# First expert layer with its weight blocks stationary at run-time addresses, instead of tokens stationary

## The chip, the cores and the metric

The kernel runs on one core of a Trainium2 chip. The metric is the device time in microseconds (us), median of several executions. A ratio compares a kernel with the kernel before on the same chip, and uses fast runs only; where numbers of two chips stand side by side, the text says so. With one core, "slow" only means a run more than 1.5% above the fastest run of the same kernel. For a kernel whose runs spread more widely, the fast ratio therefore flatters, and the median of all runs is given beside it.

## The reference, cut to what matters

```python
# attention with random features: q, k, v are 8 batches x 8 heads x 576 x 64
# -> x, 8 x 576 tokens of D = 512
e = argmax(x @ w_gate)                 # or the token before's expert, if a local gate says so
h = np.maximum(x[b, s] @ w1[e], 0.0)   # w1: 8 experts x 512 x 1024
out[b, s] = p[e] * (h @ w2[e])         # w2: 8 experts x 1024 x 512
```

Each token goes to one of eight experts. Which one is known only at run time. (The code in this document is shortened; `...` marks what is left out.)

## The kernel before

After attention the tokens are sorted by expert into pages of 128 tokens; 38 pages are computed. A page gathers its tokens (`xg`), turns them so that D lies on the partitions (`xt`), and loads the column offset of its expert, `ev`, into a register of TensorE. All of w1 and w2 is to lie in SBUF: `w1_all` and `w2_all`, 4,096 columns (`WE`) for each expert. There `ds(ev + ..., n)` is a slice at a run-time address. In the traces a matmul is two instructions: a weight load (LDWEIGHTS) and the matmul itself; layer 1 before has 304 LDWEIGHTS `<-xt` and as many MATMUL `pj<-w_all,xt` (291 of them recorded). The operand of the weight load is called the stationary one here (`lhsT`), the other the moving one (`rhs`).

```python
def hidden(n, xt, ev_src, mid=lambda: None):             # layer 1 of a page
    ev = nc.values_load(ev_src, engines=(PE,), ...)
    h_ps = ...                                           # PSUM, 128 tokens x 1024 units
    for c in range(2):
        for dc in range(DC):                             # DC = 4
            nc.tensor.matmul(h_ps[:, c, :], lhsT=xt[:, dc, :],                  # stationary: tokens
                             rhs=w1_all[:, ds(ev + (dc * F + c * 512), 512)],   # moving: weights
                             start=(dc == 0), stop=(dc == DC - 1))
        if c == 0:
            mid()                                        # transposes of the next page's tokens
    h = arena[:, n % 3].rearrange(...)
    nc.scalar.activation(h, h_ps..., Act.Relu)           # tokens on the partitions
    return h, ev

def hidden_t(h, n=FC):                                   # FC = 8: units onto the partitions
    ...                                                  # tp in PSUM, ht in SBUF
    for f in range(n):
        nc.tensor.transpose(tp[:, f], h[:, f], ident_bf)
    nc.vector.tensor_copy(ht[:, 0:n], tp[:, 0:n])
    if n < FC:
        nc.sync.dma_start_transpose(out=ht[:, n:], in_=h[:, n:]...)
    return ht, n_
```

Layer 2 (`output`) is eight matmuls with a 128x128 block of `ht` stationary and 512 columns of w2, also at a run-time address, moving. The first 17 pages do layer 1 only, while w2 is still being loaded (three loads of `w_load` per page); then both layers alternate. Routing ("gate", with one-hot tables built on VectorE) is done twice, once for each half of the tokens.

The softmax here doesn't subtract the row's maximum and nothing guards it: scores larger than these inputs give would overflow.

Of the kernel before, what the change touches and what calls it, by code (L numbers as in the profile page):

```python
# [23 lines left out]
NEP = 18  # L24
# [6 lines left out]
def kernel(  # L31
# [118 lines left out]
    def w_load():  # L150
        if wload and wdst[wload[0][0]] is not None:
            l, e, i = wload.pop(0)
            src = (moe_w1, moe_w2)[l]
            w = src.shape[2]
            nb = 1024 // w
            nc.gpsimd.dma_start(  # L156
                out=wdst[l][:, ds(e * WE + i * 1024, 1024)].rearrange("p (c f) -> p c f", f=w),
                in_=src[e].rearrange(("(c p) f -> p c f", "(p c) f -> p c f")[l], p=128)[:, i * nb:(i + 1) * nb, :])
# [170 lines left out]
    ids2 = consts.tile([128, 18, 2], BF)  # L329
    wt8 = consts.tile([128, E], F32)  # L330
    io128 = consts.tile([128, 128], BF)
# [9 lines left out]
    def gate_consts():  # L341
# [3 lines left out]
        nc.gpsimd.iota(io128, pattern=[[1, 128]], base=0, channel_multiplier=0, **fdt)  # L345
# [11 lines left out]
        nc.gpsimd.iota(ids2[:, :, 0].rearrange("p (a r) -> p a r", a=2), pattern=[[128, 2], [0, 9]], base=0,  # L357
                       channel_multiplier=1, **fdt)
        nc.gpsimd.iota(ids2[:, :, 1].rearrange("p (a r) -> p a r", a=2), pattern=[[0, 2], [1, 9]], base=1,
                       channel_multiplier=0, **fdt)  # L360
        nc.gpsimd.iota(wt8, pattern=[[-1, E]], base=E, channel_multiplier=0, **fdt)
        nc.gpsimd.iota(cpg, pattern=[[1, NC]], base=0, channel_multiplier=0, **fdt)
        yield
# [18 lines left out]
    def gate(ep, gt, n):  # L382

# [73 lines left out]
        slf, col = t18("slf"), t18("col")  # L457
        nc.vector.tensor_copy(slf, slot)
        if ep == 0:
            nc.vector.tensor_copy(col, gpg)  # L460
        else:
            nc.vector.tensor_scalar(col, gpg, scalar1=float(NEP), scalar2=over, op0=Alu.is_ge, op1=Alu.mult)
            nc.vector.tensor_tensor(col, col, gpg, op=Alu.add)
# [4 lines left out]
        oh, pg = t18("oh", 128, BF), t18("pg", NC, BF)  # L468
        ri = gt.tile([128, n, 2, NC], BF, name="ri")

        def parts(r_, v_, t_):
            shape = list(r_.shape)
            nc.vector.tensor_tensor(r_, pg[:, t_].unsqueeze(2).to_broadcast(shape), v_[:, t_].unsqueeze(3).to_broadcast(shape),
                                    op=Alu.mult)

        def build(g):
            t_ = slice(n * g, n * g + n)
            nc.vector.tensor_tensor(oh[:, t_], io128.unsqueeze(1).to_broadcast([128, n, 128]),
                                    slf[:, t_].to_broadcast([128, n, 128]), op=Alu.is_equal)
            nc.vector.tensor_tensor(pg[:, t_], cpg.unsqueeze(1).to_broadcast([128, n, NC]),  # L480
                                    col[:, t_].to_broadcast([128, n, NC]), op=Alu.is_equal)
            parts(ri, ids2, t_)
# [4 lines left out]
        for g in range(18 // n):  # L487
            for i in range(n):
                nc.tensor.matmul(l_ps.rearrange("p a c -> p (a c)"), lhsT=oh[:, n * g + i],
                                 rhs=ri[:, i].rearrange("p a c -> p (a c)"),  # L490
                                 start=(g == 0 and i == 0), stop=(n * g + i == 17))
            yield
            if n * (g + 1) < 18:
# [36 lines left out]
        lists[ep] = dict(idr=idr, ix=ix, lid=lid, tmp=(ex, fr, m_, rs, oh, pg, parts))  # L530

    def both(ep, n):
        yield from gate(ep, gt, n)
        yield from probs(ep, gt)

    def probs(ep, gt):

        ex, fr, m_, rs, oh, pg, parts = lists[ep].pop("tmp")
# [5 lines left out]
        v3, pr = t18("v3", 3, BF), t18("pr")  # L544
        rp = gt.tile([128, 6, 3, NC], BF, name="rp")
# [5 lines left out]
        for i in range(2):  # L551
            nc.vector.tensor_copy(v3[:, :, i:i + 1], pr)
            nc.vector.tensor_tensor(v3[:, :, 2:3] if i else pr, pr, v3[:, :, i:i + 1], op=Alu.subtract)
# [4 lines left out]
        for g in range(3):  # L558
            parts(rp, v3, slice(6 * g, 6 * g + 6))
            yield  # L560
            for i in range(6):
                nc.tensor.matmul(p_ps.rearrange("p a c -> p (a c)"), lhsT=oh[:, 6 * g + i],
                                 rhs=rp[:, i].rearrange("p a c -> p (a c)"),
# [40 lines left out]
    outs, hs, done, spare = [], {}, [], list(range(3, 9))  # L604
    NST = 2 * NEP + 2

    def hidden(n, xt, ev_src, mid=lambda: None):
        ev = nc.values_load(ev_src, engines=(PE,), min_val=0, max_val=(E - 1) * WE,
                            skip_runtime_bounds_check_because="multiples of the columns of one expert")
        h_ps = ps_p.tile([128, 8, 128], F32, name="pj").rearrange("p (a x) c -> p a (x c)", a=2)  # L610
        for c in range(2):
            for dc in range(DC):
                nc.tensor.matmul(h_ps[:, c, :], lhsT=xt[:, dc, :], rhs=w1_all[:, ds(ev + (dc * F + c * 512), 512)],  # L613
                                 start=(dc == 0), stop=(dc == DC - 1))
            if c == 0:
                mid()
        h = arena[:, n % 3].rearrange("p (f c) -> p f c", c=128)
        nc.scalar.activation(h, h_ps.rearrange("p a x -> p (a x)").rearrange("p (c f) -> p f c", f=FC), Act.Relu)  # L618
        return h, ev

    def hidden_t(h, n=FC):

        tp = ps_t.tile([128, FC, 128], BF, name="tp")
        for f in range(n):
            nc.tensor.transpose(tp[:, f], h[:, f], ident_bf)  # L625
        n_ = spare.pop(0) if spare else 0
# [243 lines left out]
```

## Time and profile before

| | before |
|---|---|
| time, median | 333.0 us |
| profiled span; mean granted clock of TensorE | 330.9 us; 0.903 |
| first layer-1 matmul | 155.9 us |
| first layer-2 matmul | 217.8 us |
| start of the last matmul | 320.9 us |
| layer-1 and layer-2 matmuls at full clock, start to start | 216 ns each |

Two lines of the page of the kernel before. The first is the granted clock in forty slices of the span, in tenths (9 is 90% or more). The second is the group of layer-1 matmuls: count, then busy time and mean ns of one, then the idle time ahead of them.

```profile
PEclk9859779999899959555799997999999999999996
...
L613 PE MATMUL pj<-w_all,xt 128*128 x291 | 75.2, 389 | 2.6 <-ACT xt L599 1.4
```

In the second half of the span the clock is full nearly throughout, and layer 1 has almost no idle time ahead of it (2.6 us in all). The mean of 389 ns is the latency of a pipelined matmul, whose end the profile models; the pace is the distance between starts, 216 ns. (13 of the 304 records are missing.)

### The profile page before, as it was taken

What the parts mean: (1) busy time and instruction counts of PE and PEld (TensorE: products, weight loads), DVE (VectorE), ACT (ScalarE), POOL (GpSimd) and SP (SyncE); (2) the same over time, 40 slices, a digit from 0 to 9 for tenths busy, and PEclk for the clock granted to TensorE, in tenths of its full rate; (3) what the DMA queues carried; (4) which work ended last, traced back from release to release, by engine and by line L of the source; (5) the groups of instructions that cost most, each with busy time, mean ns of one, the idle gap of its engine ahead of it and who ended that gap; (6) DMA issues with size and microseconds to landing.
All of it is one profiled execution on the core that took longest, in us unless ns stands there. A gap on an engine that the chain in (4) does not pass through costs nothing. (4 is left out here: it accounts for less than half of the span.)

```text
span 330.9 us, 7843 instructions
## 1 busy us (share of the span) xinstructions
PE 257.2 (78%) x2789; PEld 151.7 (46%) x2809; DVE 183.2 (55%) x406; ACT 154.1 (47%) x230; POOL 195.8 (59%) x299
## 2 busy tenths in 40 slices
PE   2585488768787775722998885999999999999980
PEld 1464256546464553411565453554444444444430
DVE  2677188788879768980354776423333333323440
ACT  1586498888889865510555452532122221222000
POOL 3677787698498595356377653325555657432550
PEclk9859779999899959555799997999999999999996
DMA  7999989999888789999689996338668666532330
GB/s 230 391 411 408 315 238 326 368 271 301 285 239 259 239 150 202 224 223 222 130 167 206 226 226 164 81 82 184 171 173 176 189 148 171 168 112 79 129 133 32
DMA packets 52649, 69.89 MB, mean 211 GB/s; under 512 B 25552, under 2 KB 27088, under 8 KB 52608
## 3 DMA queue, kind: packets, MB, share of 16 engines
q0 software_dynamic: 14176, 31.14, 42.4%
q1 hardware_dynamic: 34352, 33.43, 30.9%
q10 hardware_dynamic: 4080, 4.77, 4.2%
q8 instruction: 26, 0.43, 0.5%
q14 instruction: 15, 0.12, 0.1%
HBM read 67.16 MB, written 14.68 MB: 247 GB/s over the span
## 5 line engine op out<-in xcount | busy, mean ns | idle before, releaser
L613 PE MATMUL pj<-w_all,xt 128*128 x291 | 75.2, 389 | 2.6 <-ACT xt L599 1.4
L618 ACT ACTIVATE arena<-pj 128x1024 bf16<-128x1024 f32 x38 | 38.9, 1023 | 75.3 <-PE pj L613 70.9
L644 POOL DMA_INDIRECT out_dram<-y,idr x38 | 37.8, 995 | 51.3 <-DVE y L643 47.3
L584 POOL DMA_INDIRECT xg<-x_tok,ix x36 | 37.4, 1038 | 27.3 <-PE tp L597 16.5
L212 DVE TENSOR_REDUCE kmx<-pj 128x8 f32<-128x1024 f32 x36 | 44.0, 1222 | 16.1 <-ACT kvb L251 8.4
L232 POOL TENSOR_TENSOR va<-vs,ek 128x512 bf16<-128x512 f32 (+1 forms) x40 | 38.2, 958 | 21.0 <-ACT ek L221 15.3
L156 POOL DMA_DIRECT2D w_all<-in_moe_w_dram x64 | 35.8, 565 | 16.4 <-DMA w_all<-in_moe_w_dram 15.3
L281 ACT ACTIVATE qp<-pj 128x1024 bf16<-128x1024 f32 x36 | 37.5, 1043 | 12.4 <-PE pj L275 12.3
L613 PEld LDWEIGHTS <-xt 128*128 128x128 bf16 x304 | 29.0, 99 | 30.2 <-issue 2.2
L218 ACT ACTIVATE kp<-pj 128x1024 bf16<-128x1024 f32 x36 | 37.3, 1037 | 11.2 <-DVE kmx L212 11.2
L643 DVE TENSOR_SCALAR y<-po,prb 128x512 f32<-128x512 f32 x24 | 18.0, 751 | 29.0 <-PE po L638 29.0
L183 PE MATMUL tp<-ident_bf,kb 128*128 128x128 bf16 x144 | 17.1, 246 | 17.1 <-POOL kb L110 8.1
L206 PE MATMUL pj<-om_bd,kt 128*128 128x256 bf16 x144 | 25.8, 310 | 2.9 <-ACT qp L281 1.8
L305 DVE TENSOR_TENSOR xr<-po,rd 128x512 bf16<-128x512 f32 x36 | 24.9, 692 | 1.2
L599 ACT COPY xt<-tp 128x512 bf16<-128x512 bf16 x18 | 10.5, 584 | 30.2 <-PE tp L597 29.1
L638 PE MATMUL po<-w_all,ht 128*128 x103 | 24.5, 379 | 0.1
L628 DVE COPY ht<-tp 128x1024 bf16<-128x1024 bf16 (+1 forms) x20 | 11.9, 597 | 22.5 <-PE tp L625 22.5
L116 POOL CAST qb<-arena 128x512 bf16<-128x512 f32 x36 | 21.1, 612 | 3.9 <-DMA arena<-in_q_dram 3.9
L729 ACT COPY qt<-tp 128x512 bf16<-128x512 bf16 x36 | 21.6, 601 | 3.6 <-DVE kt L727 2.7
L638 PEld LDWEIGHTS <-ht 128*128 128x128 bf16 x160 | 15.1, 98 | 16.1
L628 DVE COPY arena<-tp 128x512 bf16<-128x512 bf16 (+1 forms) x18 | 9.2, 514 | 22.0 <-PE tp L625 22.0
L727 DVE COPY kt<-tp 128x512 bf16<-128x512 bf16 x36 | 15.0, 417 | 11.3 <-PE tp L183 11.2
(152 smaller groups left out, 394.7 us busy)
## 6 DMA issues: line engine op xcount, KB each, us to landing
w_all<-in_moe_w_dram POOLq DMA_DIRECT2D x64, 256.0 KB, 7.9
vs<-in_v_dram SPq DMA_DIRECT2D x8, 1152.0 KB, 12.5
arena<-in_q_dram SPq DMA_DIRECT2D x4, 2304.0 KB, 15.1
ks<-in_k_dram SPq DMA_DIRECT2D x7, 1152.0 KB, 13.8
x_tok<-xr ACTq DMA_DIRECT2D x16, 256.0 KB, 5.7
ks<-in_k_dram SPq DMA_DIRECT2D x1, 640.0 KB, 5.6
out_dram<-y,idr POOLq DMA_INDIRECT x38, 2.9
xg<-x_tok,ix POOLq DMA_INDIRECT x36, 3.7
```

Of the source, the lines that this page charges most:

```text
L156: nc.gpsimd.dma_start(out=wdst[l][:, ds(e * WE + i * 1024, 1024)].rearrange("p (c f) -> p c f", f=w), in_=src[e].rearrange(("(c p) f -> p ...
L206: nc.tensor.matmul(pj[:, 2 * i:2 * i + 2, :].rearrange("p a d -> p (a d)"), lhsT=kts[t][:, i], rhs=om_bd, start=True, stop=True)
L212: nc.vector.tensor_reduce(mx, kpj[t], axis=AX, op=Alu.max)
L218: nc.scalar.activation(kp, kpj.pop(t), Act.Exp, scale=scale)
L232: nc.gpsimd.tensor_tensor(va[:, x, 0:Dh].rearrange("p (r h) d -> p r h d", h=4), vv, ek[:, x].rearrange("p (r h) o -> p r h o", h=4).to_br ...
L281: nc.scalar.activation(qp, qpj.pop(s), Act.Exp, scale=scale)
L305: nc.vector.tensor_tensor(xrs[s][:, u % 2, :].rearrange("p (g h d) -> p g h d", g=2, h=4), ov[:, :, :, 0:Dh], rd.to_broadcast([128, 2, 4, ...
L584: nc.gpsimd.indirect_dma_start(out=xg, out_offset=None, in_=src, in_offset=bass.IndirectOffsetOnAxis(ap=ix, axis=0), bounds_check=TE - 1, ...
L613: nc.tensor.matmul(h_ps[:, c, :], lhsT=xt[:, dc, :], rhs=w1_all[:, ds(ev + (dc * F + c * 512), 512)], start=(dc == 0), stop=(dc == DC - 1))
L618: nc.scalar.activation(h, h_ps.rearrange("p a x -> p (a x)").rearrange("p (c f) -> p f c", f=FC), Act.Relu)
L638: nc.tensor.matmul(y_ps[:, 0, :], lhsT=htn[0][:, f], rhs=w2_all[:, ds(ev + f * D, D)], start=(f == 0), stop=(f == FC - 1))
L644: s_ = nc.gpsimd.indirect_dma_start(out=out_flat, out_offset=bass.IndirectOffsetOnAxis(ap=idr[:, c:c + 1], axis=0), in_=y, in_offset=None, ...
```

## The change

Its intent: if the weight blocks are stationary and the 128 tokens move, layer 1 comes out with the units on the partitions, which is what layer 2 needs. So the transposes, their copies and their DMA transposes go. The array's work for a page stays about the same: 32 matmuls of 128 columns; 8 of 512 columns, 216 ns apart in the trace before, make 1.73 us.

```diff
-        for c in range(2):
+        for f in range(FC):
             for dc in range(DC):
-                nc.tensor.matmul(h_ps[:, c, :], lhsT=xt[:, dc, :], rhs=w1_all[:, ds(ev + (dc * F + c * 512), 512)],
-                                 start=(dc == 0), stop=(dc == DC - 1))
-            if c == 0:
+                nc.tensor.matmul(h_ps[:, f], lhsT=w1_all[:, ds(ev + (dc * F + f * 128), 128)],
+                                 rhs=xt[:, dc, :], start=(dc == 0), stop=(dc == DC - 1))
+            if f == 3:
                 mid()
...
-    def hidden_t(h, n=FC):            # whole function goes
...
# w2 is read with the order of units that layer 1 now gives: 2 KB rows instead of 4 KB
-    in_=src[e].rearrange(("(c p) f -> p c f", "(p c) f -> p c f")[l], p=128)[:, i * nb:(i + 1) * nb, :])
+    in_=src[e].rearrange("(c p) f -> p c f", p=128)[:, i * nb:(i + 1) * nb, :])
...
# routing tables: all operands 16-bit, innermost step 1 (six tokens innermost)
-        oh, pg = t18("oh", 128, BF), t18("pg", NC, BF)
+        oh = gt.tile([128, 3, 128, 6], BF, name="oh")
+        pg = gt.tile([128, 3, NC, 6], BF, name="pg")
...
-                nc.tensor.matmul(l_ps..., lhsT=oh[:, n * g + i], ...)
+                nc.tensor.matmul(l_ps..., lhsT=oh[:, g, :, i], ...)     # elements of oh, and of the moving ri, now 12 bytes apart
...
# some casts of k a step earlier; two weight loads per step instead of three before the first pages
-            t = max(9 * P + d_, i - 2) if g == 0 else 9 * P + d_
+            t = max(9 * P + d_, i - 2) if g == 0 else 9 * P + d_ - (P > 0 and i == 1)
-            for _ in range(3 if 0 not in lists else 0):
+            for _ in range(2 if 0 not in lists else 0):
...
# and: two more pauses in the second routing; a page's h is ready for layer 2 one page earlier
```

More of the change, by code (lines that the diff above doesn't have):

```diff
@@ L328 @@
     rmask = consts.tile([128, 2, 9], F32)
-    ids2 = consts.tile([128, 18, 2], BF)
+    ids2 = consts.tile([128, 2, 18], BF)
     wt8 = consts.tile([128, E], F32)
-    io128 = consts.tile([128, 128], BF)
+    io6 = consts.tile([128, 128, 6], BF)
+    cpg6 = consts.tile([128, NC, 6], BF)
     cpg = consts.tile([128, NC], F32)
@@ L344, in gate_consts @@
         nc.gpsimd.tensor_tensor(ident2, ident[:, 0:64], ident[:, 64:128], op=Alu.add)
-        nc.gpsimd.iota(io128, pattern=[[1, 128]], base=0, channel_multiplier=0, **fdt)
+        nc.gpsimd.iota(io6, pattern=[[1, 128], [0, 6]], base=0, channel_multiplier=0, **fdt)
         yield
@@ L356, in gate_consts @@
         yield
-        nc.gpsimd.iota(ids2[:, :, 0].rearrange("p (a r) -> p a r", a=2), pattern=[[128, 2], [0, 9]], base=0,
+        nc.gpsimd.iota(ids2[:, 0].rearrange("p (a r) -> p a r", a=2), pattern=[[128, 2], [0, 9]], base=0,
                        channel_multiplier=1, **fdt)
-        nc.gpsimd.iota(ids2[:, :, 1].rearrange("p (a r) -> p a r", a=2), pattern=[[0, 2], [1, 9]], base=1,
+        nc.gpsimd.iota(ids2[:, 1].rearrange("p (a r) -> p a r", a=2), pattern=[[0, 2], [1, 9]], base=1,
                        channel_multiplier=0, **fdt)
@@ L362, in gate_consts @@
         nc.gpsimd.iota(cpg, pattern=[[1, NC]], base=0, channel_multiplier=0, **fdt)
+        nc.gpsimd.iota(cpg6, pattern=[[1, NC], [0, 6]], base=0, channel_multiplier=0, **fdt)
         yield
@@ L380, with gate @@
     lists = {}
-    def gate(ep, gt, n):
+    def gate(ep, gt):
         lg = lgs[ep]
@@ L456, in gate @@
         nc.vector.tensor_scalar(gpg, code, scalar1=7, scalar2=None, op0=Alu.logical_shift_right)
-        slf, col = t18("slf"), t18("col")
-        nc.vector.tensor_copy(slf, slot)
+        slf, col = gt.tile([128, 18], BF, name="slf"), gt.tile([128, 18], BF, name="col")
+        nc.vector.tensor_copy(slf.unsqueeze(2), slot)
         if ep == 0:
-            nc.vector.tensor_copy(col, gpg)
+            nc.vector.tensor_copy(col.unsqueeze(2), gpg)
         else:
-            nc.vector.tensor_scalar(col, gpg, scalar1=float(NEP), scalar2=over, op0=Alu.is_ge, op1=Alu.mult)
-            nc.vector.tensor_tensor(col, col, gpg, op=Alu.add)
+            cof = t18("cof")
+            nc.vector.tensor_scalar(cof, gpg, scalar1=float(NEP), scalar2=over, op0=Alu.is_ge, op1=Alu.mult)
+            nc.vector.tensor_tensor(col.unsqueeze(2), cof, gpg, op=Alu.add)
         if ep:
@@ L466, in gate, with parts @@
             yield
-        oh, pg = t18("oh", 128, BF), t18("pg", NC, BF)
-        ri = gt.tile([128, n, 2, NC], BF, name="ri")
-        def parts(r_, v_, t_):
+        oh = gt.tile([128, 3, 128, 6], BF, name="oh")
+        pg = gt.tile([128, 3, NC, 6], BF, name="pg")
+        rp = gt.tile([128, 3, NC, 6], BF, name="rp")
+        ri = rp[:, 0:2]
+        def parts(r_, v_, g):
             shape = list(r_.shape)
-            nc.vector.tensor_tensor(r_, pg[:, t_].unsqueeze(2).to_broadcast(shape), v_[:, t_].unsqueeze(3).to_broadcast(shape),
-                                    op=Alu.mult)
+            nc.vector.tensor_tensor(r_, pg[:, g].unsqueeze(1).to_broadcast(shape),
+                                    v_[:, :, 6 * g:6 * g + 6].unsqueeze(2).to_broadcast(shape), op=Alu.mult)
         def build(g):
-            t_ = slice(n * g, n * g + n)
-            nc.vector.tensor_tensor(oh[:, t_], io128.unsqueeze(1).to_broadcast([128, n, 128]),
-                                    slf[:, t_].to_broadcast([128, n, 128]), op=Alu.is_equal)
-            nc.vector.tensor_tensor(pg[:, t_], cpg.unsqueeze(1).to_broadcast([128, n, NC]),
-                                    col[:, t_].to_broadcast([128, n, NC]), op=Alu.is_equal)
-            parts(ri, ids2, t_)
+            for o_, c_, x_ in ((oh, io6, slf), (pg, cpg6, col)):
+                nc.vector.tensor_tensor(o_[:, g], c_, x_[:, 6 * g:6 * g + 6].unsqueeze(1).to_broadcast(list(c_.shape)),
+                                        op=Alu.is_equal)
+            parts(ri, ids2, g)
         build(0)
@@ L486, in gate @@
         l_ps = ps_k.tile([128, 2, NC], F32, name="kv")
-        for g in range(18 // n):
-            for i in range(n):
-                nc.tensor.matmul(l_ps.rearrange("p a c -> p (a c)"), lhsT=oh[:, n * g + i],
-                                 rhs=ri[:, i].rearrange("p a c -> p (a c)"),
-                                 start=(g == 0 and i == 0), stop=(n * g + i == 17))
+        for g in range(3):
+            for i in range(6):
+                nc.tensor.matmul(l_ps.rearrange("p a c -> p (a c)"), lhsT=oh[:, g, :, i],
+                                 rhs=ri[:, :, :, i].rearrange("p a c -> p (a c)"),
+                                 start=(g == 0 and i == 0), stop=(g == 2 and i == 5))
             yield
-            if n * (g + 1) < 18:
+            if g < 2:
                 build(g + 1)
@@ L529, in gate, with both @@
         nc.vector.tensor_scalar(over, gbs[:, E:E + 1], scalar1=float(-NEP), scalar2=over, op0=Alu.add, op1=Alu.add)
-        lists[ep] = dict(idr=idr, ix=ix, lid=lid, tmp=(ex, fr, m_, rs, oh, pg, parts))
-    def both(ep, n):
-        yield from gate(ep, gt, n)
+        lists[ep] = dict(idr=idr, ix=ix, lid=lid, tmp=(ex, fr, m_, rs, oh, rp, parts))
+    def both(ep):
+        yield from gate(ep, gt)
+        if ep:
+            yield
+            yield
         yield from probs(ep, gt)
     def probs(ep, gt):
-        ex, fr, m_, rs, oh, pg, parts = lists[ep].pop("tmp")
+        ex, fr, m_, rs, oh, rp, parts = lists[ep].pop("tmp")
         def t18(nm, w=1, dt=F32):
             return gt.tile([128, 18, w], dt, name=nm)
-        v3, pr = t18("v3", 3, BF), t18("pr")
-        rp = gt.tile([128, 6, 3, NC], BF, name="rp")
+        v3, pr = gt.tile([128, 3, 18], BF, name="v3"), t18("pr")
         nc.vector.tensor_reduce(rs, ex, axis=AX, op=Alu.add)
@@ L551, in probs @@
         for i in range(2):
-            nc.vector.tensor_copy(v3[:, :, i:i + 1], pr)
-            nc.vector.tensor_tensor(v3[:, :, 2:3] if i else pr, pr, v3[:, :, i:i + 1], op=Alu.subtract)
+            nc.vector.tensor_copy(v3[:, i].unsqueeze(2), pr)
+            nc.vector.tensor_tensor(v3[:, 2].unsqueeze(2) if i else pr, pr, v3[:, i].unsqueeze(2), op=Alu.subtract)
         if ep:
@@ L558, in probs @@
         for g in range(3):
-            parts(rp, v3, slice(6 * g, 6 * g + 6))
+            parts(rp, v3, g)
             yield
             for i in range(6):
-                nc.tensor.matmul(p_ps.rearrange("p a c -> p (a c)"), lhsT=oh[:, 6 * g + i],
-                                 rhs=rp[:, i].rearrange("p a c -> p (a c)"),
+                nc.tensor.matmul(p_ps.rearrange("p a c -> p (a c)"), lhsT=oh[:, g, :, i],
+                                 rhs=rp[:, :, :, i].rearrange("p a c -> p (a c)"),
                                  start=(g == 0 and i == 0), stop=(g == 2 and i == 5))
@@ L603, with hidden @@
     WH = 17
-    outs, hs, done, spare = [], {}, [], list(range(3, 9))
+    outs, done, spare = [], [], list(range(9))
     NST = 2 * NEP + 2
-    def hidden(n, xt, ev_src, mid=lambda: None):
+    def hidden(xt, ev_src, mid=lambda: None):
         ev = nc.values_load(ev_src, engines=(PE,), min_val=0, max_val=(E - 1) * WE,
                             skip_runtime_bounds_check_because="multiples of the columns of one expert")
-        h_ps = ps_p.tile([128, 8, 128], F32, name="pj").rearrange("p (a x) c -> p a (x c)", a=2)
-        for c in range(2):
+        h_ps = ps_p.tile([128, FC, 128], F32, name="pj")
+        for f in range(FC):
             for dc in range(DC):
-                nc.tensor.matmul(h_ps[:, c, :], lhsT=xt[:, dc, :], rhs=w1_all[:, ds(ev + (dc * F + c * 512), 512)],
-                                 start=(dc == 0), stop=(dc == DC - 1))
-            if c == 0:
+                nc.tensor.matmul(h_ps[:, f], lhsT=w1_all[:, ds(ev + (dc * F + f * 128), 128)],
+                                 rhs=xt[:, dc, :], start=(dc == 0), stop=(dc == DC - 1))
+            if f == 3:
                 mid()
-        h = arena[:, n % 3].rearrange("p (f c) -> p f c", c=128)
-        nc.scalar.activation(h, h_ps.rearrange("p a x -> p (a x)").rearrange("p (c f) -> p f c", f=FC), Act.Relu)
-        return h, ev
-    def hidden_t(h, n=FC):
-        tp = ps_t.tile([128, FC, 128], BF, name="tp")
-        for f in range(n):
-            nc.tensor.transpose(tp[:, f], h[:, f], ident_bf)
-        n_ = spare.pop(0) if spare else 0
-        ht = arena[:, n_].rearrange("p (f c) -> p f c", c=128) if n_ else moh.tile([128, FC, 128], BF, name="ht")
-        nc.vector.tensor_copy(ht[:, 0:n], tp[:, 0:n])
-        if n < FC:
-            nc.sync.dma_start_transpose(out=ht[:, n:], in_=h[:, n:].rearrange("p f c -> p (f c)"))
-        return ht, n_
+        n_ = spare.pop(0) if spare else None
+        ht = (moh.tile([128, FC, 128], BF, name="ht") if n_ is None
+              else arena[:, n_].rearrange("p (f c) -> p f c", c=128))
+        nc.scalar.activation(ht, h_ps, Act.Relu)
+        return (ht, n_), ev
     def output(pg, htn, ev, last=False):
@@ L639, in output @@
                              start=(f == 0), stop=(f == FC - 1))
-        if htn[1]:
+        if htn[1] is not None:
             spare.append(htn[1])
@@ L673, in gate_part @@
                 next(ga, None)
-        if j < NST:
-            hs[j] = hidden(j, xts.pop(j), pages[j][1], mid)
+        done.append((pages[j],) + hidden(xts.pop(j), pages[j][1], mid))
         gate_part()
-        if j >= 1:
-            h, ev = hs.pop(j - 1)
-            done.append((pages[j - 1], hidden_t(h, FC // 2 if NEP <= j < NST - 1 else FC), ev))
         gate_part()
@@ L799 @@
             gt = pool("gt", 1, side="right", **rw)
-            ga = both(0, 6)
+            ga = both(0)
             next(ga)
@@ L812 @@
     mo2 = pool("mo2", 4, **rw)
-    moh = pool("moh", WH - 5, **rw)
-    ga = both(1, 6)
+    moh = pool("moh", WH - 8, **rw)
+    ga = both(1)
     next(ga)
-    for j in range(early[0], NST + 1):
+    for j in range(early[0], NST):
         page(j, 3, True)
@@ L833, in rest @@
                 pg = pages[2 * NEP + i + d]
-                h, ev = hidden(d, turn(fetch(pg[0])), pg[1])
-                output(pg, hidden_t(h), ev)
+                ht, ev = hidden(turn(fetch(pg[0])), pg[1])
+                output(pg, ht, ev)
             if i + 2 < NOV:
```

## The prediction

> **What bounds the kernel now.** I read four views: the stretches by engine, the waits, the order of instructions in time, and single lines of the program inside short windows.
>
> Stretches (us; busy time and count of PE, PEld, DVE, ACT, POOL; clock; DMA share; GB/s):
> ```profile
> core 0: us, PE busy (x) PEld busy (x) DVE busy (x) ACT busy (x) POOL busy (x), PEclk, DMA share, GB/s
> 140.00:150.00 10.00, 2.59 (x36) 1.51 (x30) 7.51 (x26) 2.27 (x3) 5.40 (x7) 0.50 1.12 220
> 150.00:160.00 10.00, 4.50 (x19) 2.36 (x21) 0.00 (x0) 1.18 (x3) 6.09 (x8) 0.50 0.81 187
> ...
> 190.00:200.00 10.00, 7.81 (x68) 4.42 (x68) 7.77 (x26) 4.83 (x6) 5.73 (x9) 1.00 1.12 225
> ...
> 220.00:240.00 20.00, 19.89 (x107) 9.63 (x108) 6.84 (x12) 4.46 (x5) 11.22 (x11) 1.00 0.69 169
> ```
> Attention runs to about 145 us. Then comes a hole (PE 2.6 and 4.5 of 10 us busy). Up to about 213 us the first 17 pages of 128 tokens pass through expert layer 1 only, while w2 still streams in. From 213 us PE is full at clock 1.00 until 321 us, so there the time of a page on PE is the time of the kernel. The last 9.6 us (321.3 to 330.9) are the last store and the end.
>
> Two waits:
> ```profile
> PE tp L597 <- DMA xg<-x_tok,ix: 7.2, 1, 7.2
> PE tp L597 <- DVE ht L628: 4.3, 2, 3.7
> ```
> The first is the hole: the first gather queues behind weight loads. The second is PE standing behind DVE near 199 us, because the copy of transposed activations is queued behind DVE's routing chain.
>
> A late page in order of time:
> ```profile
> 228.57 1.89 PE L613 MATMUL pj<-w_all,xt 128*128 x8
> 230.30 0.39 PE L625 MATMUL tp<-ident_bf,arena 128*128 128x128 bf16 x4
> 230.52 1.89 PE L638 MATMUL po<-w_all,arena 128*128 x8
> ```
> Start to start: layer 1 takes 1.73 us (8 matmuls of 512 columns at 216 ns), four transposes 0.22 us (55 ns each, each with its own weight load), layer 2 1.73 us. The change is aimed at those transposes.
>
> What decides, I think, is one line seen in two windows and one for comparison (first: a static stream; then layer 1's register instructions as the first page starts; last: the load of the expert's offset):
> ```profile
> 128.38 0.35 PEld L291 LDWEIGHTS <-qp 128*64 128x64 bf16 x16 [0.23 <-DVE ni L445]
> ...
> L613 PEldq FUSED_REGOPS  x8: 42/46/51, 155.8 to 156.7; - x8
> ...
> L608 PEldq TENSOR_LOAD <-ei x38: 296/303/592, 155.2 to 298.0; - x38
> ```
> Every matmul whose weights lie at a run-time offset has one register instruction ahead of it on PE's sequencer: 304 for layer 1 (38 pages x 8), 304 for layer 2. When nothing holds the sequencer, eight of them start within 0.89 us, 0.9/7, near 124 ns apart (the records behind the line: 349 of 607 gaps are 122 to 126 ns). That is the sequencer's price for register instruction, weight load and matmul. PE's clock was 0.5 there and a matmul took 427 ns, and in the late pages the same 124 ns stands beside 216 ns matmuls, so the array does not set it. Where addresses are fixed, 16 weight loads with their matmuls pass in 0.35 us, 22 ns a pair. So the dynamic address costs about 100 ns. Today that is hidden, since 124 is less than 216.
>
> [...]
>
> **The change part by part.**
> Transposes and their copies: 228 transposes x 55 ns = 12.6 us leave PE, 38 DVE copies (597 and 514 ns) leave DVE, and 19 DMA transposes go. The 3.7 us wait goes too, and layer 1 feeds layer 2 one page earlier.
> Layer 1 on the array: 32 matmuls x 55 = 1.77 us a page against 1.73: +1.6 us in all.
> Layer 1 on the sequencer: 32 register instructions where there were 8. If the dynamic weight load costs what the dynamic matmul does, 32 x 124 = 3.97 us a page, over twice the array's 1.77. With the offset load (0.4 us to the next register instruction) and four fixed transposes (0.1), a layer-1 page takes 4.5 us; each layer 2 takes the sequencer 8 x 124 = 0.99 us.
> [...]
> Two weight loads per step instead of three before the gather: about 14 instead of 21 loads from 120 us on. A load is 128 packets at 175 ns on 16 engines, 1.4 us, so the backlog before the gather shrinks and it lands 3 to 4 us sooner. In total layer 1 starts near 149.5 us instead of 155.2. Earlier casts of k: perhaps 1 us, inside that.
> w2 in 2 KB rows: 256 descriptors a load instead of 128, the same bytes; I take 0 to 10% per load. About 28 loads are left for pages 5 to 14, three a page, 4.2 us at today's rate: below the 4.5 of the sequencer.
>
> Sum: 17 pages x 4.5 = 77, so page 17 at 226 us (today 213.7). Then 21 pages with 31 layer-2 passes between them: 21 x 4.42 + 31 x 0.99 = 124 us of sequencer (the array needs only 21 x 1.77 + 31 x 1.73 = 91). Reached: 350. Seven layer-2 passes are left at array pace, 12: 362. End 9.6: 371.6 of span, plus the 2.1 us by which the median time (333.0) exceeds the profiled span: 374 us.
>
> **Rivals.**
> (A) The sequencer keeps up: a weight load with a register address is cheap, below about 70 ns with its register instruction. For it: the hardware may treat it otherwise than a matmul, and nothing in this trace has a dynamic weight load; all the side changes (DVE, backlog, DVE wait) aim rightly at what the profile shows, as one would tune a version that gained. Then pages 5 to 14 are DMA-bound at 4.2 us, page 17 comes near 205, and the rest is array-bound: 21 x 1.77 + 38 x 1.73 = 103, plus 9.6 and 2.1: 320 us.
> (B) 2 KB rows make w2 the bound. DMA share is already 1.12 at 190 to 200 us. If a load took twice as long, 28 x 2.8 = 78 us from 152 put the start of layer 2 at 230 and the end at 345. Against it: k's 2,304 B packets take about 97 ns and w's 4 KB reads 175, so time goes nearly with bytes.
> (C) With the array busy only 55 of each 124 ns the clock could drop to half. Layer 2 would then take 3.4 us and the time pass 400. [...]
>
> **Range and chances.** The outcome has two humps: the sequencer's near 374 (355 to 390) and the array's near 320. I give the first two chances in three, since its 124 ns is measured but for a dynamic matmul, not a dynamic weight load; the second a bit over one in four; little lies between. The range must span both: 316 to 392. Faster by over 2%: 0.27; within: 0.06; slower: 0.67.
>
> **What would show it.** 1216 register instructions for layer 1, about 124 ns apart; layer-1 matmuls 124 ns apart with PE gaps put down to issue; 4.4 us a page after 226. Right on the side parts: [...]the wait for the first gather down from 7.2 to 4 us or less, no copy of ht on DVE. I am wrong if layer-1 matmuls stand 55 to 80 ns apart: then rival A, and the end near 320. If POOL waits for w2 grow beyond 2 us each, rival B.

The forecast's sum came to 371.6 us of span and 374 us of time. The part on routing on VectorE with its term of -2.5 us is in the numbers: the start of layer 1 near 149.5 us is 155.2 less the 3 to 4 us of the backlog and these 2.5 us, and 374 builds on that start.

## The result, and the profile after

| | before | after |
|---|---|---|
| time, median of 4 | 332.95 us (332.22 to 334.21) | 490.3 us (488.27 to 492.06) |
| span; clock | 330.9 us; 0.903 | 487.9 us; 0.752 |
| first layer-1 matmul | 155.9 us | 144.3 us |
| first layer-2 matmul | 217.8 us | 281.9 us |
| start of the last matmul | 320.9 us | 474.8 us |

The ratio is 1.472, 95% interval 1.464 to 1.479; the four runs before lie within 0.6%. Ratios here are the mean time of one kernel's fast runs over that of the other's of the same rounds, so not quite the ratio of the medians quoted.

The page of the changed kernel: the clock in slices, then layer 1's matmuls and weight loads.

```profile
PEclk9598998997855555555555569887989889698795
...
L618 PE MATMUL pj<-xt,w_all 128*128 128x128 bf16 x1216 | 227.5, 247 | 8.8 <-issue 2.2
L618 PEld LDWEIGHTS <-w_all 128*128 x1216 | 117.6, 104 | 117.2 <-issue 19.8
```

The clock is at half over twelve slices in a row; in the records it is from 129.5 to 286.5 us, and after that again in short stretches, mostly of 3.4 us. Layer 1 has grown from 75.2 to 227.5 us of "busy" time, but a matmul counts as busy for its whole latency, 247 ns in the mean, while the next one starts after 208 ns (below); the busy share says that something is in flight, not that the array works.

The stretches by engine of the changed kernel (the columns are those of the same view in the prediction):

```profile
140.00:150.00 10.00, 7.43 (x53) 4.19 (x52) 2.00 (x5) 2.20 (x3) 2.17 (x3) 0.50 0.34 101
150.00:160.00 10.00, 7.87 (x56) 4.63 (x56) 1.50 (x4) 2.63 (x3) 4.78 (x6) 0.50 0.66 130
190.00:200.00 10.00, 9.68 (x51) 5.14 (x50) 0.49 (x2) 2.16 (x3) 5.69 (x8) 0.50 0.67 113
220.00:240.00 20.00, 19.92 (x113) 11.52 (x113) 3.12 (x15) 4.52 (x6) 6.33 (x8) 0.50 0.62 95
```

The hole at 150 us is smaller (7.87 us busy where it was 4.50), so the start did get earlier. But from 190 to 200 us, 9.68 us busy hold only 51 matmuls, 46 of them layer 1's: one in 196 ns. VectorE is busy for 0.49 of these 10 us, ScalarE for 2.16, GpSimd for 5.69, and the DMA share has fallen from 1.12 to 0.67: none of them is busy throughout.

What TensorE waits for is in the view of single lines; "PEldq" is how the profile marks instructions of TensorE's sequencer, FUSED_REGOPS being the register instructions. The register instructions of layer 1 over the whole run, then in a window with page 7, then the load of the expert's offset (durations are min/median/max in ns):

```profile
L618 PEldq FUSED_REGOPS  x2432: 37/46/51, 143.6 to 458.3; - x188
...
L618 PEldq FUSED_REGOPS  x64: 42/46/51, 200.5 to 207.3; - x64
...
L613 PEldq TENSOR_LOAD <-ei x38: 297/302/531, 143.0 to 451.1; - x38
```

There are 2,432 register instructions, two for each of 1,216 matmuls: in the order of the records one stands ahead of the weight load and one ahead of the matmul (why the matmul, whose own moving operand is fixed, has one too is not shown). A page has 64 of them, and they take 6.8 us from first to last, with transposes for the next page among them. In the records behind the line the median gap is 104 ns, so a matmul starts every 208 ns. The median distance of layer-1 matmuls is 208 ns both where the granted clock is 0.5 and where it is 1.0. So the clock does not set that pace, nor does the array: where it does, in fixed_addr below, the same matmuls are 56 ns apart at full clock and 107 at half.

A late page in order of time (start, us, engine, line, operation):

```profile
419.81 3.19 PE L618 MATMUL pj<-xt,w_all 128*128 128x128 bf16 x15
...
422.91 3.49 PE L633 MATMUL po<-w_all,arena 128*128 x8
...
428.05 3.99 PE L618 MATMUL pj<-xt,w_all 128*128 128x128 bf16 x30
```

Here layer 2 takes 3.49 us for eight matmuls, twice its time before: the clock is at half in this place. Of 283 gaps between layer-2 matmuls below 1 us, 95 lie at half clock with a median of 426 ns; the other 188 keep 216 ns.

The side parts. The wait for the first gather, after:

```profile
PE tp L601 <- DMA xg<-x_tok,ix: 1.9, 1, 1.9
```

It was 7.2 us. And the one-hot builds on VectorE, before and after (groups with different shapes kept apart):

```profile
L478 DVE TENSOR_TENSOR oh<-io,slf 128x768 bf16<-128x768 bf16 x6 | 5.7, 950 | 0.0
```

```profile
L482 DVE TENSOR_TENSOR oh<-io,slf 128x768 bf16<-128x768 bf16 x6 | 3.4, 561 | 0.0
```

950 ns have become 561, the page tables 352 to 249, the id parts 558 to 358.

### The profile page after: what moved, and what is told of

Read it like the earlier page. It is cut to its first block, busy times and chain, and to the rows that moved or that the text cites. A ratio compares the mean times of both kernels' runs of the same rounds, so it can differ in the third digit from the quotient of the medians.

```text
span 487.9 us, 11274 instructions
## 1 busy us (share of the span) xinstructions
PE 422.0 (87%) x3493; PEld 237.6 (49%) x3493; DVE 158.5 (32%) x368; ACT 153.7 (32%) x230; POOL 204.6 (42%) x300
## 5 line engine op out<-in xcount | busy, mean ns | idle before, releaser
L618 PE MATMUL pj<-xt,w_all 128*128 128x128 bf16 x1216 | 227.5, 247 | 8.8 <-issue 2.2
L618 PEld LDWEIGHTS <-w_all 128*128 x1216 | 117.6, 104 | 117.2 <-issue 19.8
L625 ACT ACTIVATE arena<-pj 128x1024 bf16<-128x1024 f32 x26 | 26.6, 1024 | 155.3 <-PE pj L618 155.3
L156 POOL DMA_DIRECT2D w_all<-in_moe_w_dram x64 | 41.5, 660 | 14.2 <-PE pj L618 8.7
L633 PE MATMUL po<-w_all,arena 128*128 x128 | 42.7, 494 | 0.2 <-issue 0.2
L633 PEld LDWEIGHTS <-arena 128*128 128x128 bf16 x208 | 23.1, 111 | 31.2 <-issue 16.0
L603 ACT COPY xt<-tp 128x512 bf16<-128x512 bf16 x18 | 10.5, 586 | 63.1 <-PE tp L601 63.1
L625 ACT ACTIVATE ht<-pj 128x1024 bf16<-128x1024 f32 x12 | 12.3, 1024 | 48.7 <-PE pj L618 48.7
L206 PE MATMUL pj<-om_bd,kt 128*128 128x256 bf16 x144 | 24.8, 301 | 3.0 <-ACT qp L281 1.6
L633 PE MATMUL po<-w_all,ht 128*128 x64 | 21.9, 504 | 0.0
L183 PEld LDWEIGHTS <-kb 128*128 128x128 bf16 x144 | 11.2, 108 | 19.9 <-issue 8.1
## 6 DMA issues: line engine op xcount, KB each, us to landing
vs<-in_v_dram SPq DMA_DIRECT2D x8, 1152.0 KB, 13.1
```

Of the source, the lines that this page charges most:

```text
L156: nc.gpsimd.dma_start(out=wdst[l][:, ds(e * WE + i * 1024, 1024)].rearrange("p (c f) -> p c f", f=w), in_=src[e].rearrange("(c p) f -> p c ...
L183: nc.tensor.transpose(tp[:, w, i], source(t, nm, i).rearrange("p h d -> p (h d)"), ident_bf)
L618: nc.tensor.matmul(h_ps[:, f], lhsT=w1_all[:, ds(ev + (dc * F + f * 128), 128)], rhs=xt[:, dc, :], start=(dc == 0), stop=(dc == DC - 1))
L625: nc.scalar.activation(ht, h_ps, Act.Relu)
L633: nc.tensor.matmul(y_ps[:, 0, :], lhsT=htn[0][:, f], rhs=w2_all[:, ds(ev + f * D, D)], start=(f == 0), stop=(f == FC - 1))
```

## The experiments

Theory 1, from the trace: the register instructions of the run-time weight addresses are the whole loss, two per matmul at 104 ns each. Theory 2, the rival: the loss is in the small matmuls themselves (four times as many of a quarter of the width) or in the half clock. A second rival puts part of it on the side changes or on the 2 KB rows. The runs came with the kernel before beside it: median 336.2 us in the first four, 336.9 in the next four, 338.0 in the last two.

### fixed_addr: the same matmuls, address known at compile time

```diff
-   lhsT=w1_all[:, ds(ev + (dc * F + f * 128), 128)]
+   lhsT=w1_all[:, dc * F + f * 128:dc * F + f * 128 + 128]
```

Every page reads expert 0 in layer 1: a wrong result, with the same work.

> The changed kernel with one edit: layer 1 reads expert 0's weights at a fixed address for every page (wrong result on purpose; layer 2 keeps its run-time offset). Theory 1 (the register instructions, two per layer-1 matmul at 104 ns each, set the pace): the 2432 register instructions of layer 1 vanish, its matmuls stand about 55 to 60 ns apart, PE's clock goes back to 1.00, and the time falls from 490 us to 305 to 325 us. Theory 2 (128-column matmuls with a new weight block each are slow on the array, or the half clock is the cause and not the effect): the time stays above 420 us.

Measured: 325.3 us (324.13 to 325.5), ratio to before 0.966 (0.961 to 0.971), clock 0.89. There is no register instruction in layer 1. A late page in order of time:

```profile
243.54 1.99 PEld L618 LDWEIGHTS <-w_all 128*128 128x128 bf16 x32
243.76 1.95 PE L618 MATMUL pj<-xt,w_all 128*128 128x128 bf16 x32
...
245.54 1.89 PE L633 MATMUL po<-w_all,ht 128*128 x8
```

All 32 matmuls of a page start within 1.78 us (243.76 to 245.54), 56 ns apart at full clock (in the whole run 1,091 of 1,125 gaps of layer 1 at full clock are 55 to 56 ns). Width and number of the matmuls are those of the changed kernel, and the ratio to before has gone from 1.472 to 0.966. Theory 2 falls as the whole explanation. The time is at the upper edge of what was expected (305 to 325). The load of w2 now holds the kernel up for a while: TensorE's layer 2 waits for it four times, 4.2 us in all, from 201.6 us on, and ahead of that the DMA share is at 1.23 (1.12 before, from 190 to 200 us):

```profile
180.00:190.00 10.00, 7.23 (x104) 6.86 (x102) 5.17 (x23) 4.83 (x6) 7.57 (x10) 0.87 1.23 223
190.00:200.00 10.00, 7.81 (x109) 7.11 (x107) 1.20 (x5) 3.32 (x5) 7.20 (x10) 0.96 1.23 220
```

In these stretches TensorE is busy 7 to 8 us of 10 while the DMA share stands at 1.23. (Reading one expert only could also spare waits for w1; copy_early below, with the right weights, leaves that aside.)

### l1_alone: only the new layer 1 and its w2 order

```diff
# the kernel before, with hidden(), the removal of hidden_t() and the 2 KB rows of the change;
# routing, casts of k and the number of weight loads as before
```

> The kernel before with nothing but the new layer 1 (and w2 in 2 KB rows, which it needs). Theory 1: the whole loss is there, so 495 to 510 us, the changed kernel's 490 plus the 10 to 15 us that the other edits gain. Rival (part of the loss comes from the other edits): clearly under 490 us.

Measured: 498.6 us (497.69 to 499.23), ratio 1.482 (1.474 to 1.489), clock 0.745.

```profile
L614 PEldq FUSED_REGOPS  x2432: 37/46/51, 156.4 to 468.3; - x188
```

The same 2,432 instructions, again 104 ns apart in the median, and 208 ns from matmul to matmul at both clocks. The whole loss sits in layer 1 with its w2 order. Against the full change it starts 13 us later (156.4 instead of 143.6 us). How much of that the side parts keep to the end the two comparisons do not settle: the profiled spans differ by 9.3 us (497.2 and 487.9), while the ratios to before differ by only 0.010 (1.482 and 1.472, some 3 us), because the kernel before took 336.2 us on this chip and 333.0 on the other. In between the two kernels keep the same pace: from page 17 to page 37 (counted from 0) both take 178.2 us.

### sides: everything but the new layer 1

```diff
# the changed kernel, with hidden(), hidden_t() and w2's 4 KB rows of the kernel before;
# routing, casts and two loads per step stay as changed
```

> The changed kernel with layer 1 put back as before (weights moving, transposes, w2 in 4 KB rows) and all other edits kept (routing layout, two weight loads a step, earlier casts, the two extra pauses). Theory 1: these gain what the trace of the changed kernel shows, layer 1 starting near 143 us instead of 155, so 316 to 324 us against 333. Rival: the early start is eaten up again because w2's loads, now later, hold the pages; then 328 to 335 us.

Measured: 332.5 us (327.74 to 336.31), ratio 0.977 (0.971 to 0.984) from the two of its four runs that were in the fast state, which is unclear at the limit of 2%; by the medians of all runs it is 0.989. The profiled run was slow, and its clock (0.901) is that of a fast run of the kernel before. The rival number held, not mine of 316 to 324. One line of each kernel points to the reason (issues of weight loads: durations, then the first and the last start). Before:

```profile
L156 POOL DMA_DIRECT2D w_all<-in_moe_w_dram x64: 527/572/768, 37.0 to 195.0; - x64
```

and with the side changes:

```profile
L156 POOL DMA_DIRECT2D w_all<-in_moe_w_dram x64: 530/572/766, 37.4 to 205.4; - x64
```

The gather comes earlier with fewer weight loads ahead of it (from 119.5 us on, 11 are issued before the first gather at 135.1 us in the changed kernel, 21 before that at 145.3 us in the kernel before), but those loads have to be made later: the last one goes out at 205.4 instead of 195.0 us (202.1 in the fast profile of the same kernel, sides_again).

### moving128: narrow matmuls with one register instruction

```diff
# the kernel before; weights stay the moving operand
-   for dc in range(DC):
-       nc.tensor.matmul(h_ps[:, c, :], lhsT=xt[:, dc, :], rhs=w1_all[:, ds(ev + (dc * F + c * 512), 512)], ...)
+   for s in range(4):
+       for dc in range(DC):
+           nc.tensor.matmul(h_ps[:, c, s * 128:s * 128 + 128], lhsT=xt[:, dc, :],
+                            rhs=w1_all[:, ds(ev + (dc * F + c * 512 + s * 128), 128)], ...)
```

> The kernel before with layer 1's moving weights cut into 128-column pieces: 32 matmuls a page with fixed weight loads and a run-time offset on the moving side, so one register instruction per matmul instead of two. Theory 1 (count of register instructions): about 124 ns per matmul, 4.0 us per layer 1, 375 to 400 us in all, half way to the changed kernel. Theory 2 (a weight load at a run-time address is what is slow): the pieces run at the array's 55 ns and the time stays within 333 to 345 us.

Measured: 394.9 us (393.0 to 396.28), ratio 1.173 (1.166 to 1.180), clock 0.922.

```profile
L614 PEldq FUSED_REGOPS  x1216: 42/46/51, 157.5 to 365.3; - x174
```

One register instruction per matmul, a median of 124 ns from one to the next and from matmul to matmul, about 4.0 us a page. This is the pace that the prediction read from the kernel before and used for the new layer 1. It is right for a run-time moving operand. From 161 to 386 us the clock is full here, although the array works only 56 of every 124 ns. In the changed kernel it works 107 of every 208 ns at half clock and 56 of 208 at full clock. (These shares are estimates: 56 and 107 ns are the median gaps at full and half clock in fixed_addr.)

So the dose is: no register instruction, 56 ns; one on the moving side, 124; the two of a stationary operand, 208.

### moving128_load: what the 124 ns consist of

```diff
# moving128, with one more weight load at a fixed address ahead of each matmul
+           nc.tensor.ldweights(xt[:, DC - 1 - dc, :])
            nc.tensor.matmul(...)
```

> The kernel before with layer 1 cut in 128 columns (one register instruction per matmul, 124 ns apart in the run moving128) and one more weight load at a fixed address ahead of each matmul. If TensorE's sequencer takes about 84 ns per register instruction and 20 ns per tensor instruction, which fits 124 = 84 + 2x20 and 208 = 2x(84 + 20): the layer-1 matmuls come 144 ns apart, the page 4.6 us, time about 394.9 + 38x32x0.020 = 419 us. Rival (the pace is a fixed figure of the matmul with its register instruction, extra weight loads go by unseen): 124 ns and about 395 us. [...]

Measured: 395.1 us in a single look, its state unknown. The weight loads of the added line and the register instructions of the old:

```profile
L614 PEld LDWEIGHTS <-xt x1216: 95/96/147, 154.6 to 365.0; 128*128 128x128 bf16 x174
```

```profile
L615 PEldq FUSED_REGOPS  x1216: 42/46/51, 154.9 to 365.2; - x174
```

1,216 more weight loads, and still 124 ns in the median and the same time as moving128. My split of the pace into 84 ns for a register instruction and 20 ns for each tensor instruction falls: one more weight load with a fixed address passes at no cost here. The rival holds.

### both_run_time: a second run-time operand on each matmul

```diff
# the changed kernel (reads weights instead of tokens: wrong on purpose)
-   rhs=xt[:, dc, :]
+   rhs=w1_all[:, ds(ev + (dc * F + f * 128), 128)]
```

> The changed kernel with the moving operand at a run-time address too (it reads weights instead of tokens: a wrong result on purpose). If each register instruction costs about 104 ns in the sequencer whatever it serves: three per matmul make 312 ns, a page of 10 us, about 490 + 38x32x0.104 = 617 us; if the two operands share one, two per matmul, 208 ns and about 490 us. Rival (the pace is set by the run-time weight load itself, not by register instructions): 208 ns whatever their number.

Measured: 532.0 us in a single look, its state unknown.

```profile
L618 PEldq FUSED_REGOPS  x2432: 42/56/83, 144.5 to 498.7; - x188
```

There are still two register instructions per matmul (the two operands are at the same place; whether that is why is not shown), yet the matmuls stand 241 to 242 ns apart (median, at full and half clock), which neither number foresaw. In the records the register instructions themselves have become unequal: the one ahead of a weight load takes 46 or 51 ns, the one ahead of a matmul 79 or 74. The gap to the next is the instruction's own time plus 58 to 59 ns, here (46 to 104, 51 to 109, 74 to 133, 79 to 138) as in the changed kernel (46 to 104). The 34 ns more per matmul, times 38x32, are 41 us, close to the difference to the 490.3 us of the changed kernel (on another chip). So the number of register instructions alone is not the price either: with a second register-held operand the one ahead of the matmul is longer (79 or 74 ns, 46 in the changed kernel). A weight load at a run-time address standing alone, ahead of a fixed matmul, would have told what one such load costs; no run tried that form, so this stays open.

### sides_2k and sides_again: the 2 KB rows

```diff
# sides_2k: as sides, but w2 in 2 KB rows (units in natural order); sides_again: the same kernel as sides
```

> The old layer 1 and all other edits of the change, with w2 read in 2 KB rows instead of 4 KB; compare with sides_again in the same rounds. If the w2 load sets the pace from about 150 to 205 us: 13 per cent more time per byte (2 packets of 98 ns against one of 173 to 175 ns in the earlier runs) over some 60 us at most makes it 3 to 8 us slower than sides_again. Rival (the load is hidden behind layer 1, as the prediction held): within 1.5 us of sides_again.

> The same kernel as in the run sides, so that sides_2k has its neighbour in the same rounds: 328 to 336 us, ratio to before 0.97 to 0.985.

Measured: sides_2k 334.2 us (329.73 to 336.17), ratio 0.985 (0.978 to 0.992) from three fast runs of six; sides_again 332.9 us (330.73 to 338.81), ratio 0.988 (0.983 to 0.993) from five of six. By the medians of all runs they are 0.992 and 0.988. The intervals overlap and the fast ratios lie 0.3% apart, the 2 KB rows ahead, so the cost of 3 to 8 us did not come and the rival held, although POOL takes longer to issue a load. First 2 KB rows, then 4 KB:

```profile
L156 POOL DMA_DIRECT2D w_all<-in_moe_w_dram x64: 528/701/801, 37.5 to 201.7; - x64
```

```profile
L156 POOL DMA_DIRECT2D w_all<-in_moe_w_dram x64: 527/574/763, 37.6 to 202.1; - x64
```

The median issue takes 701 instead of 574 ns, but the last load goes out at about the same time. sides_again also shows the fate of the earlier start: layer 1 begins at 148.6 us, 7.3 us before that of the kernel before (155.9), but layer 2 at 216.3, only 1.5 us before (217.8). The two profiles are from different chips.

### copy_w1: right result, most addresses fixed

The loss belongs to addresses in TensorE's instructions, so VectorE, busy for 0.49 of 10 us from 190 to 200 us in the changed kernel, can take the run-time address instead: one copy per half page into a fixed tile.

```diff
+   ec = nc.values_load(..., engines=(DVE,), ...)
+   wc = wcp.tile([128, DC, F // 2], BF)          # two tiles of 4 KB per partition
+   nc.vector.tensor_copy(wc, w1_all[:, ds(ec, WE)]...[:, :, k * (F // 2):(k + 1) * (F // 2)])
-   lhsT=w1_all[:, ds(ev + (dc * F + f * 128), 128)]
+   lhsT=wc[:, dc, f % 4 * 128:f % 4 * 128 + 128]  # from page 6 on
```

> The changed kernel, but VectorE copies each page's w1 columns (two halves of 128x4x512) out of the run-time place into one of two fixed tiles, half a page ahead of TensorE, from the second half of the pages on; so most layer-1 matmuls have no register instruction, and the result is right. Theory (register instructions are the whole loss): layer-1 matmuls 56 ns apart at full clock, no register instruction among them except in the first pages, time 325 to 335 us, near the 325.3 us of the wrong-on-purpose fixed-address kernel plus some waits for copies. Rival (the copies, behind the routing work in VectorE's line, become the wait): over 340 us, with TensorE waiting for VectorE in most pages.

Measured: 355.4 us (352.54 to 357.99), ratio 1.055 (1.050 to 1.061). The number is the rival's (over 340), but not for its reason: in the whole run TensorE waits for copies three times, 7.3 us. The lines of layer 1:

```profile
L631 PE MATMUL pj<-xt,wc x1024: 217/219/314, 194.9 to 326.4; 128*128 128x128 bf16 x171
L631 PEldq FUSED_REGOPS  x384: 37/46/51, 145.7 to 194.4; - x192
```

The copied pages run at 56 ns per matmul from 194.9 us on. The first six pages, for which there was no room for the tiles, still have 2x32 register instructions each and last until 194.4 us, some 8 us a page.

### copy_early: right result, all addresses fixed

```diff
# the two tiles lie in four of the nine slots of the arena, which is free when the pages start
-   WH = 17                                        # pages that do layer 1 only
+   WH = 16                                        # (so in copy_w1 too)
-   spare = list(range(9))
+   spare = list(range(5))
+   wc = arena[:, 5 + 2 * k:7 + 2 * k]...
```

> As copy_w1, but the two fixed tiles lie in the first-stage buffer that is free when the pages start, so every page from the first reads copied weights; the result is right. Theory (in copy_w1 the first six pages, still at 208 ns per matmul and 7.4 us apart, cost what it lost against the fixed-address kernel): no register instruction in layer 1 at all, matmuls 56 ns apart at full clock, time 326 to 336 us (fixed-address kernel 325.3 on another day, plus copies on VectorE of 0.7 us each behind the second half's routing). Rival (the copies' waits, 7.3 us of TensorE idle in copy_w1, grow in the early pages where VectorE still routes): over 340 us.

Measured: 333.0 us (329.08 to 334.22), ratio 0.981 (0.976 to 0.987), correct. No register instruction is left in layer 1. The copies on VectorE, and the longest wait of TensorE for them:

```profile
L620 DVE COPY arena<-w_all x76: 673/695/966, 144.4 to 301.1; 128x2048 bf16 x76
```

```profile
PE pj L631 <- DVE arena L620: 11.7, 6, 3.0
```

76 copies of 695 ns, each with one register instruction on VectorE, stand for 2,432 register instructions on TensorE. TensorE waits for them six times, 11.7 us in all, five of the six before layer 2 begins at 210.6 us; how much of that would otherwise have been a wait for w2 is not shown. By the ratios this kernel needs a third less time than the changed one (0.981 against 1.472), and 1.9% less than the kernel before (1.5% by the medians of all runs; unclear at the limit of 2%). It does not beat the side changes with the old layer 1 beyond what the intervals allow (0.977 and 0.988), and falls short of the 0.966 that the wrong kernel with fixed addresses reaches.

## Why the prediction was wrong

The direction and the mechanism were right: register instructions on TensorE's sequencer bound layer 1, the array did not, and the change lost. The time of 374 us was 116 us too low, and 490 lies far outside the range.

**The step that failed** is "32 register instructions where there were 8. If the dynamic weight load costs what the dynamic matmul does, 32 x 124 = 3.97 us a page". There are 64 of them a page, not 32, since a run-time stationary operand has one ahead of its weight load and one ahead of its matmul. They stand 104 ns apart, so a page has 32 x 208 = 6.66 us. The difference, 32 x 84 ns = 2.69 us a page, times 38 pages, is 102 of the 116 us. Fixed addresses show it by absence (fixed_addr, 56 ns), and moving128 shows that 124 ns was right for the case it had been read from. The prediction named the assumption itself ("its 124 ns is measured but for a dynamic matmul, not a dynamic weight load"), but opened the range mostly downward (316 to 392 around 374): a weight load cheaper than assumed was a rival, one dearer was not. A reading beside it was off, without weight: the 22 ns a pair of the fixed-address stream counts the last load's own length; from start to start it is 16 to 18 ns.

**The sum by stages.** The prediction has page 17 (counted from 0) at 226 us and the last matmul at 362; the trace has 274.9 and 474.8.

| stage | predicted | measured | of it 2.69 us a page | left |
|---|---|---|---|---|
| start of layer 1 | 149.5 | 144.3 | | -5.2 |
| 17 pages of layer 1 only | 77 | 130.6 | 45.7 | +7.9 |
| from page 17 to the last matmul | 136 | 199.9 | 56.5 | +7.4 |
| last matmul to the end | 9.6 | 13.1 | | +3.5 |

Of the 7.9 us, 4.5 are the first two pages: they start 8.8 and 10.5 us ahead of the next, the later ones mostly 7.4; attention's last work stands among them, and the second page waits 2.0 us for a weight load to land. The 7.4 us of the second stage may be the half clock: 95 layer-2 matmuls 210 ns longer are 20 us at most, partly beside work of the sequencer. No run took the clock away alone, so this share is not shown. The 3.5 us at the end were not looked into.

**The chances** of 0.67 for slower were well placed: the mechanism of the first hump was the right one, though the time lies 100 us above its upper end. The mass for rival A, that the sequencer keeps up with run-time weight loads, was not: 208 ns is nearly four times the 56 ns of fixed_addr.

**Rival C** happened: the clock dropped at 129.5 us, during the routing (TensorE busy for 3.73 of the 6.5 us ahead of it) as in the kernel before (at 133.5 us, 3.55 of 7.0), and did not come back when layer 1 began, but 157 us after the drop. The forecast's argument against it had read the trace of the kernel before too kindly: attention, too, has half clock there, from 38.0, 89.2 and 116.5 us. The case it was named for, the array working some 55 of every 124 ns, is moving128, and there the clock was full from 161 to 386 us; with a matmul every 208 ns it stayed at half until 286.5 us. What releases the clock is not shown. But the clock is not the cause of the loss, as layer 1's pace is 208 ns at either clock.

**Rival B** did not: the rows of 2 KB are within 0.3% of the 4 KB rows (sides_2k beside sides_again), and POOL's waits for weight loads, which would have shown it, fell from 15.3 us before (19 times, 1.8 at most) to 5.5 (5 times, 1.7 at most). Per byte, packets became about 13% dearer where the DMA share is 1.12 or more: two of 98 ns in fixed_addr against one of 173 ns before (medians from 180 to 200 us). The prediction had 0 to 10%.

**The side parts** went as predicted or better in their own terms: the gather's wait 1.9 us (4 or less), start 144.3 (149.5). On VectorE the builds took 561 ns (950 before), the page tables 249 (352), the id parts 358 (558). The new layout has a price on TensorE: with 64 moving columns the routing's matmuls started 91 ns apart (sides_again; 92 in the trace after; 29 before, contiguous, both at full clock), with 96 columns 133 (43 before at full clock, 80 at half). The 32 more columns cost 42 ns, 1.3 ns each; before they cost 14 ns at full clock, 0.4 each, and 28 at half, 0.9 each. So with the moving operand's elements 12 bytes apart each column took longer; what the same step in the weights costs is not shown. The prediction did not follow their worth for the whole time to the end: the loads held back before the gather return as a later w2. In sides they were worth 2.3% by the fast runs and in sides_again 1.2% (1.1% and 1.2% by the medians of all runs), and with the old layer 1 most of the earlier start was gone by layer 2.

**Removing the transposes** was worth little. The array's work in layer 1 is the same either way (32 x 56 = 1.79 us against 8 x 216 = 1.73), so the gain could be no more than the transposes' 12.6 us and the wait for their copies. With the addresses fixed and the waits of copy_early, the kernel is where the side changes alone are. Without those waits, in fixed_addr (0.966, wrong result), it is 1 to 2% below the two runs of the side changes.

## What to carry to other kernels

Before moving an operand with a run-time address to the other side of a matmul, or cutting it finer, count the sequencer's instructions: here a price of 124 ns, hidden behind 216 ns of array work, was bare behind 56. A price measured for one form of an instruction is an estimate for another form, so its range must be open in both directions. If the address is the cost, let an idle engine take it once per page (76 copies here) rather than TensorE once per matmul, and when work is delayed to start a stage earlier, follow it to where it comes back.
